# When an attention row's operands are asked for and copied, in a fused attention and MoE kernel

## The chip, the cores and the metric

The kernel runs on one core of a Trainium2 chip. The core has TensorE (PE: matrix products into PSUM), VectorE (DVE), ScalarE (ACT) and GpSimd (POOL), and SyncE (SP), which here only issues DMAs. The metric is the device time of one execution in microseconds, taken as the median over runs; lower is better.

## The reference

The inputs are q, k and v of 8 batch rows x 8 heads x 576 positions x 64, and two weight matrices. Attention is causal within a window: the first four heads see the last 32 positions ("sliding"), the other four every fourth of the last 128 ("dilated"). The result goes through a two-layer network with a squared ReLU.

```python
rel = pos[:, None] - pos[None, :]
mask_plain = (rel >= 0) & (rel < window)                     # window = 32
mask_dil = (rel >= 0) & (rel < window * dilation) & (rel % dilation == 0)   # dilation = 4
scores = np.where(masks, scale * q @ k.T, -1e9)
attn = exp(scores - max) / (sum + 1e-09)
x = (attn @ v).transpose(0, 2, 1, 3).reshape(4608, 512)
h = x @ w_in                                                 # 512 x 2048
r = np.maximum(h, 0.0)
out = (r * r) @ w_out                                        # 2048 x 512
```

## The kernel before

Attention is worked row by row (b = 0 to 7), the network in nine chunks (c = 0 to 8) of 512 tokens. While TensorE works on row b, it also works on chunk b - 1. The order of every engine's instructions is written out by hand: `moe_gen` is a Python generator that emits a few matmuls per step, and `pump(n)` takes n steps. So the program alternates a piece of attention with n steps of a chunk. A chunk's first product (L299) has 32 steps; its ReLU is on ScalarE (L322, `rt`), the square on VectorE (L323, `g`). From chunk 2 on the second product (L376, `mm2_strassen_gen`) is built of seven half-size products, with sums of `g` (`gs`) on VectorE; during chunk 1's first product VectorE also makes sums of w_out (`wt`, L349). Chunks 0 and 1 use plain products (L442), and `store` copies each 128 tokens to `ot` and sends it off.

A row's path to TensorE from row 2 on:

- `load_sliding_qk` (L112): GpSimd's DMA queue loads the sliding heads' k and q from fp32 into the fp16 tile `ns`. `keep_dilated_qk` (L207) copies the dilated heads' k and q to a fp16 DRAM tile `dd`.
- `by_token` (L120) reorders `ns` into `nr`, on VectorE, for row 2 on GpSimd. `keep_sliding_qk` (L217) writes `nr` to a DRAM tile `dp`.
- `transpose_sliding` (L225) and `transpose_dilated` (L229) bring `dp` and `dd` back transposed, as `QKTp` and `QKTd`; each has two buffers, by the row's parity.
- v is loaded by SP into `sv` and `sd` (L132, L137), cast by GpSimd into `vp` and `vd` (L169, L177). A block of queries also needs the end of the block ahead, its halo: copied between partitions by ScalarE for rows 0 and 1 (`halo_sliding` L184, `halo_dilated` L189), by an SP DMA from row 2 on (L194, L197).

`attn_scores` (two sliding parts, two dilated) makes the scores (L562, L581), ScalarE their exponential, VectorE the mask (L552, L553). After each part it may call a hook, then pumps. `attn_values` multiplies by v (sliding L611, dilated L627); VectorE normalizes each product (`rcp`, `xs`, `xd`, L594 and L599). The PSUM tiles of scores and products share a pool of two buffers (`pa`), so a third product waits for the normalization of the first. For rows 2 and 3 (as 0 and 1) `x` is transposed on TensorE; from row 4 on `attn_values_by_dma` has SP transpose it (L669, L676), and calls `then[0]` and `then[1]` on the way.

In the loop over b, before:

- `after_transposes(b)` has GpSimd read one element of row b's transposed tile, so that its queue waits for the transposes to land; then GpSimd asks for row b + 1's `ns` and `dd`. So these are asked for at the start of row b's work.
- The hook behind the fourth score part (`turn`) copies `ns` to `nr`, writes `dp` and loads row b + 1's `sv`.
- For b of 4 and more, `turned` (behind two dilated products) transposes `dp`; `done` (behind the fourth) transposes `dd`, loads `sd`, has GpSimd wait for the last transposed x (L854), cast `sv` and lets SP move the sliding halo.

Each engine runs its queue in order, and an SP or GpSimd DMA waits where it stands for its operands. The tag "n" of `natp` has two buffers, taken in turn by `ns` and `nr`; `otp` has three.

Of the kernel before, what the change touches and what calls it, by code (L numbers as in the profile page):

```python
# [13 lines left out]
P = 128  # L14
# [3 lines left out]
def kernel(  # L18
# [9 lines left out]
    nc = tc.nc  # L28
# [88 lines left out]

    def by_token(b, n):
        r = natp.tile([P, 9, HH, D], FP16, name=f"nr{b}", tag="n")
        (nc.gpsimd if b == 2 else nc.vector).tensor_copy(  # L120
            r.rearrange("x j h d -> x h j d"), n.rearrange("x h (j d) -> x h j d", d=D)
        )
        return r
# [15 lines left out]
    def load_v(b):  # L139
        load_sliding_v(b)  # L140
        load_dilated_v(b, nc.sync)
# [90 lines left out]
    seen = const.tile([P, 1], FP16, name="seen")  # L232

    def after_transposes(b):
        t = QKTp[b % 2][:, 0, 1, PADP : PADP + 1] if b == 2 else QKTd[b % 2][:, 0, 1, KPAD : KPAD + 1]
        nc.gpsimd.tensor_copy(seen, t)


    nsd = {0: load_qk(0)}
# [208 lines left out]
        )  # L448

    halves = {}  # L450

    def store(c, t, po):
        if t % 2 == 0:
            halves[c] = otp.tile([P, 2, DM], FP32, name=f"ot{c}_{t}", tag="ot")
        ot = halves[c][:, t % 2]
        nc.scalar.copy(ot, po)
        (nc.sync if c else nc.gpsimd).dma_start(out=out[(c * 4 + t) * P : (c * 4 + t + 1) * P, :], in_=ot)

    def mm2_gen(c, g):
        for t in range(TOKC // P):  # L460
# [40 lines left out]
    def pump(n):  # L501
        for _ in range(n):
            while pending:
                try:
                    next(pending[0])
                    break
                except StopIteration:
                    pending.pop(0)
# [92 lines left out]
    def x_tiles(b):  # L601
        x = xp.tile([QB, 2, NB, 2, D], FP16, name=f"xs{b}", tag="xs")
        return x, [xp.tile([QD[t], DIL, HH, D], FP16, name=f"xd{b}_{t}", tag=f"xd{t}") for t in range(2)]
# [18 lines left out]
    def av_dilated(b, t, a, xs):  # L622
        pav = pa(f"paw{b}_{t}_{a}")
        for e in range(2):
            for h in range(HH):
                off = e * 288 + a * CL + Q0D[t]
                nc.tensor.matmul(  # L627
                    pav[:, e, h * (D + 2) : h * (D + 2) + D + 1],
                    AT[:, 4 + h, off : off + P],
                    vd[b % 2][:, t, 2 * a + e, h, 0 : D + 1],  # L630
                    start=True,
                    stop=True,
                )
        normalize(b, f"d{t}_{a}", pav, QD[t], xs[1][t][:, 2 * a : 2 * a + 2])
# [26 lines left out]
    def x_from(b, t, y):  # L661
        t0 = b * S % XW + DIL * Q0D[t]
        o = xT[:, 2:4, t0 : t0 + DIL * QD[t]].rearrange("x c (i r) -> x c i r", r=DIL)
        nc.scalar.copy(o, y.rearrange("x r c i -> x c i r"))  # L664
# [16 lines left out]
    def attn_scores(b, gap, less=0, hooks={}):  # L681
        for hp in range(2):
            s_sliding(b, hp)
            if hp in hooks:
                hooks[hp]()
            pump(gap)
        for g in range(2):
            s_dilated(b, g)
            if 2 + g in hooks:
                hooks[2 + g]()  # L690
            if g and b < 2:
                halo_sliding(b, 0)
            pump(gap - less)

    def attn_values(b, gap, wide=False, hooks={}):
        xs = x_tiles(b)
        for mp in range(3):
            av_sliding(b, mp, xs)
            if b < 2:
                if mp < 2:  # L700
                    halo_sliding(b, mp + 1)
                else:
                    halo_dilated(b, 0)
            pump(gap)
        x_sliding(b, 0, xs, wide)
        if b < 2:
            halo_dilated(b, 2)
        pump(gap)
        av_dilated(b, 0, 0, xs)
        pump(gap)  # L710
        x_sliding(b, 1, xs, wide)
        pump(gap)
        av_dilated(b, 0, 1, xs)
        pump(gap)
        for a in range(2):
            av_dilated(b, 1, a, xs)
            pump(gap)
        x_dilated(b, 0, xs, wide)
        pump(gap)
        x_dilated(b, 1, xs, wide)  # L720

    def attn_values_by_dma(b, then):
        xs = x_tiles(b)
        for mp in range(3):
            av_sliding(b, mp, xs)
            pump(3)
        x_sliding_by_dma(b, xs)
        ys = []
        for t in range(2):
            for a in range(2):  # L730
                av_dilated(b, t, a, xs)
                pump(4 + 2 * (a > t))
            if t == 0:
                then[0]()
            ys.append(x_dilated_by_dma(b, t, xs))
        then[1](ys[1])
        pump(6)
        x_from(b, 0, ys[0])
        pump(7)
        x_from(b, 1, ys[1])  # L740

# [35 lines left out]
    load_v(1)  # L777
    cast_sliding_v(1)
    load_w_out((3,))
    cast_dilated_v(1)  # L780
    ns = load_sliding_qk(2)
    dd = keep_dilated_qk(2)
    nr = by_token(2, ns)
    for mp in (1, 2):
        av_sliding(0, mp, xs)
        pump(1)
# [26 lines left out]
        t_dilated(1, m, a, True)  # L813
        pump(2)
    attn_scores(1, 2, 1)
    attn_values(1, 1, True)
    pump(1000)
    dp = keep_sliding_qk(2, nr)
    transpose_dilated(2, dd)
    transpose_sliding(2, dp)  # L820
    load_v(2)


    for b in range(2, B):
        pending.append(moe_gen(b - 1))
        nxt = b + 1
        hooks = {}
        if nxt < B:
            after_transposes(b)
            ns = load_sliding_qk(nxt)  # L830
            if b == 2:
                cast_v(b)
                halo_sliding_by_dma(b)
                halo_dilated_by_dma(b)
            dd = keep_dilated_qk(nxt)
        if b > 4:
            cast_dilated_v(b)
            halo_dilated_by_dma(b)
        kept = []

        def turn():
            kept.append(keep_sliding_qk(nxt, by_token(nxt, ns)))
            load_sliding_v(nxt)

        def turned():
            if nxt < B:
                transpose_sliding(nxt, kept[0])

        def done(y):
            if nxt < B:  # L850
                transpose_dilated(nxt, dd)
                if b > 3:
                    load_dilated_v(nxt, nc.sync)
                    nc.gpsimd.tensor_copy(seen, y[:, 0, 0, 0:1])  # L854
                    cast_sliding_v(nxt)
                    halo_sliding_by_dma(nxt)

        if nxt < B:
            hooks[3] = turn
        pump({2: 24, 3: 16}.get(b, 3))  # L860
        attn_scores(b, 4 if b == 2 else 3, 0, hooks)
        if b < 4:
            load_dilated_v(nxt, nc.sync)
            turned()
            done(None)
            cast_v(nxt)
            halo_sliding_by_dma(nxt)
            halo_dilated_by_dma(nxt)
            attn_values(b, b)
        else:  # L870
            attn_values_by_dma(b, (turned, done))
        pump(1000)
    pending.append(moe_gen(B - 1))
    pending.append(moe_gen(B))
# [31 lines left out]
```

## Time and profile before

| what | value |
|---|---|
| median of 13 runs | 309.73 us (307.33 to 314.84) |
| profiled execution: its time, its span | 307.95 us, 306.2 us |
| TensorE busy | 287.3 us (94%) |
| VectorE, ScalarE, GpSimd busy | 207.7, 170.5, 66.9 us |
| L299, first product, 640 matmuls | 134.0 us busy |
| `nr` copy: VectorE, GpSimd | 0.76 us (median of 5), 2.10 us (1) |
| `ns` loads, asked for to landed | 3.9 to 14.8 us, median 7.2 us |
| granted TensorE clock | 1.00 |

The profile is of one execution. A row of a timeline has the start in us, the duration in us, the engine, the line, the operation and its tiles (out<-in); in brackets stands how long the engine was idle before it and what ended that. A row of the chain has the start, the duration and the piece. Kernel stages: rows 0 and 1 and the weights until about 61 us, row 2 with chunk 1 until 95, row 3 with chunk 2 until 127, row 4 until 159, row 5 until 189, row 6 until 220, row 7 until 250, then chunks 7 and 8.

### The profile page before, as it was taken

To read this page: it belongs to the slowest core of one execution; us is meant where nothing else is said; L and a number is where in the kernel's file an instruction comes from. 1 tells how busy PE (TensorE), PEld (TensorE's weight loads), DVE (VectorE), ACT (ScalarE), POOL (GpSimd) and SP (SyncE) were. 2 spreads that over 40 slices of the span, in tenths; PEclk is the share of its full clock that TensorE was granted. 3 is DMA by queue.
4 is the path that set the end of the run, shared out by engine and by line. 5 is a ranking of instruction groups with operands and counts; after the bars stand their busy time and mean duration, and the time that the engine had idled before them with its cause. 6 is when DMAs were issued, how large, how long until landed. Compare 5 with 4: busy or idle time off the path is not lost.

```text
span 306.2 us, 6889 instructions
## 1 busy us (share of the span) xinstructions
PE 287.3 (94%) x2762; PEld 192.2 (63%) x2762; DVE 207.7 (68%) x433; ACT 170.5 (56%) x288; POOL 66.9 (22%) x117
## 2 busy tenths in 40 slices
PE   1898998999799999998999999999999999999994
PEld 0554554555355568754888987558755975785583
DVE  7784448568852698478939993899399834734652
ACT  1766648678335863494349535952595346426620
POOL 4571018413705301330044004400230000000000
PEclk9999999999999999999999999999999999999999
DMA  7899997999899989999989999999942330003004
GB/s 118 168 216 215 206 182 117 177 257 200 142 216 210 213 162 195 178 232 207 145 174 274 202 139 177 270 201 139 180 160 41 40 130 8 2 1 139 0 0 139
DMA packets 77520, 47.25 MB, mean 154 GB/s; under 512 B 58544, under 2 KB 69296, under 8 KB 77488
## 3 DMA queue, kind: packets, MB, share of 16 engines
q1 hardware_dynamic: 68416, 32.13, 50.9%
q0 software_dynamic: 9072, 14.68, 27.0%
q8 instruction: 21, 0.34, 0.5%
q14 instruction: 11, 0.09, 0.1%
HBM read 36.70 MB, written 16.52 MB: 174 GB/s over the span
## 4 chain that ended last, share of the span: by engine, by line
PE 67%; DMA 19%; DVE 4%; SPq 3%; ACT 2%; issue 2%; POOL 2%; POOLq 0%; DVEq 0%
PE ph L299 24%; PE pa L376 15%; DMA ns<-in_q_dram 12%; PE po L442 8%; PE pb L376 7%; DMA QKTd<-dd 4%; PE pc L376 3%; PE paw L627 3%; DMA sv<-in_v_dram 2%; PE pav L611 2%; PE pf L496 2%; DMA vp<-vp 2%; SPq L225 1%; SPq L229 1%; ACT AT L552 1%
## 5 line engine op out<-in xcount | busy, mean ns | idle before, releaser
L299 PE MATMUL ph<-xT,wi 128*128 128x512 f16 (+1 forms) x640 | 134.0, 359 | 0.7 <-ACT xT L664 0.7
L322 ACT ACTIVATE rt<-ph 128x512 f16<-128x512 f32 x144 | 86.2, 612 | 46.8 <-PE ph L299 40.6
L299 PEld LDWEIGHTS <-wi 128*128 128x128 f16 x640 | 68.3, 114 | 46.0 <-issue 0.6
L323 DVE TENSOR_TENSOR g<-rt 128x512 f16<-128x512 f16 x144 | 61.9, 443 | 37.7 <-ACT rt L322 37.0
L376 PEld LDWEIGHTS <-g 128*128 128x128 f16 x448 | 43.3, 98 | 6.1
L376 PEld LDWEIGHTS <-gs 128*128 128x128 f16 x336 | 31.9, 98 | 4.5 <-DVE gs L333 0.7
L442 PE MATMUL po<-wo,g 128*128 128x512 f16 x128 | 33.1, 380 | 0.0
L403 DVE TENSOR_TENSOR ov<-pb,ov 128x512 f32<-128x512 f32 x14 | 9.7, 692 | 30.7 <-PE pb L376 17.3
L376 PE MATMUL pa<-wt,gs 128*128 128x256 f16 x224 | 27.5, 273 | 0.0
L376 PE MATMUL pb<-wt,g 128*128 128x256 f16 x224 | 27.1, 273 | 0.0
L169 POOL CAST vp<-sv 128x512 f16<-128x512 f32 x24 | 14.5, 637 | 51.3 <-DMA sv<-in_v_dram 51.3
L177 POOL CAST vd<-sd 128x512 f16<-128x512 f32 (+1 forms) x32 | 22.1, 719 | 9.8 <-PE ph L299 5.2
L392 ACT COPY ov<-pa 128x512 f32<-128x512 f32 x14 | 8.2, 585 | 27.1 <-PE pa L376 27.1
L553 DVE TENSOR_TENSOR AT<-AT,maskp 128x576 f16<-128x576 f16 x32 | 19.6, 628 | 4.7 <-ACT AT L552 3.5
L599 DVE TENSOR_TENSOR xd<-paw,rcp_d 80x512 f16<-80x512 f32 (+1 forms) x32 | 21.9, 685 | 1.1
L552 ACT ACTIVATE AT<-pz 128x576 f16<-128x576 f32 x32 | 19.9, 707 | 1.7 <-PE pz L581 1.6
L552 ACT ACTIVATE AT<-ps 128x576 f16<-128x576 f32 x32 | 19.2, 660 | 1.3 <-PE ps L562 0.8
L392 ACT COPY ou<-pa 128x512 f32<-128x512 f32 x14 | 8.2, 586 | 16.6 <-PE pa L376 16.6
L599 DVE TENSOR_TENSOR xs<-pav,rcp_p 96x512 f16<-96x512 f32 x24 | 16.5, 687 | 0.8
L611 PEld LDWEIGHTS <-AT 128*128 128x128 f16 x192 | 9.0, 98 | 11.4 <-issue 5.9
L627 PEld LDWEIGHTS <-AT 128*128 128x128 f16 x256 | 11.9, 98 | 5.6 <-PE paw L627 1.3
L442 PEld LDWEIGHTS <-g 128*128 128x128 f16 x128 | 10.3, 97 | 8.1
(83 smaller groups left out, 280.1 us busy)
## 6 DMA issues: line engine op xcount, KB each, us to landing
sv<-in_v_dram SPq DMA_DIRECT2D x14, 288.0 KB, 5.7
dp<-nr SPq DMA_DIRECT2D x12, 288.0 KB, 4.0
out_dram<-ou SPq DMA_DIRECT2D x6, 512.0 KB, 3.7
out_dram<-ov SPq DMA_DIRECT2D x6, 512.0 KB, 4.6
sd<-in_v_dram SPq DMA_DIRECT2D x8, 320.0 KB, 5.3
ns<-in_k_dram POOLq DMA_DIRECT2D x8, 288.0 KB, 6.8
ns<-in_q_dram POOLq DMA_DIRECT2D x8, 288.0 KB, 7.9
sd<-in_v_dram SPq DMA_DIRECT2D x8, 256.0 KB, 6.3
```

What stands on the lines that cost most here:

```text
L177: nc.gpsimd.tensor_copy(vd[b % 2][p0:P, t, c : c + 2, :, 0:D], sd[p0:P, t, :, D * c : D * (c + 2)].rearrange("p h (c d) -> p c h d", d=D),)
L299: nc.tensor.matmul(ph[:, t0:t1], wi4[ffc // 4][:, dmk, :, ffc % 4], xT[:, dmk, x0 : x0 + t1 - t0], start=(dmk == 0 and t0 == 0), stop=(dmk ...
L322: nc.scalar.activation(rt, ph[:], ACTF.Relu)
L323: nc.vector.tensor_mul(g[:, ffc, :], rt, rt)
L376: nc.tensor.matmul(banks[bank][:, t], a(k, t), b(k), start=(new and t == 0 and k == 0), stop=(k == HF - 1), skip_group_check=True,)
L392: nc.scalar.copy(ot, banks[A])
L442: nc.tensor.matmul(po, g[:, ffc, t * P : (t + 1) * P], wo[ffc // 4][:, ffc % 4, :], start=(ffc == 0), stop=(ffc == NFF - 1),)
L552: nc.scalar.activation(AT[:, u, 0:UW], ps[:, :, 0 : UW // 2], ACTF.Exp, scale=scale)
L553: nc.vector.tensor_mul(AT[:, u, 0:UW], AT[:, u, 0:UW], mask)
L599: nc.vector.tensor_tensor(out=x, in0=pv, in1=rb, op=ALU.mult)
L611: nc.tensor.matmul(pav[:, i, h * (D + 2) : h * (D + 2) + D + 1], AT[:, 2 * (h // 2) + m // 3, off : off + P], vp[b % 2][:, m, h, 0 : D + 1 ...
L627: nc.tensor.matmul(pav[:, e, h * (D + 2) : h * (D + 2) + D + 1], AT[:, 4 + h, off : off + P], vd[b % 2][:, t, 2 * a + e, h, 0 : D + 1], st ...
```

## The change

Row 2's copy to `nr` moves from GpSimd to VectorE, in row 1's `attn_values` behind the first dilated product; its `ns` is asked for ahead of row 1's dilated casts. Row 2's sliding operands are transposed ahead of the dilated ones. Chunk 0's results no longer leave by GpSimd's queue as each is done: they are kept, and SP sends them as two stores of 512 KB behind the loads of row 2's v. Row 2's halo is copied by ScalarE, as for rows 0 and 1. Row 2's scores begin behind 18 steps of chunk 1 (24 before), row 3's behind 12 of chunk 2 (16), with 4 steps between its parts (3).

From row 5 on, `ns` and `dd` are asked for within the row ahead (`ask`): row 5's in row 3's work behind row 4's casts, row 6's and 7's in `done`, behind the casts of `sv`, with no wait for the transposes. The copy (`turn`) hangs behind the third score part in row 4 and the second in rows 5 and 6 (before: the fourth). `turned` goes ahead of the sliding products.

```diff
 def by_token(b, n):
-        (nc.gpsimd if b == 2 else nc.vector).tensor_copy(
+        nc.vector.tensor_copy(
...
+    def leave_first():
+        for t, o in first_out:
+            nc.sync.dma_start(
+                out=out[t * P : (t + 2) * P, :].rearrange("(t p) m -> p t m", p=P), in_=o
+            )
...
-        (nc.sync if c else nc.gpsimd).dma_start(out=out[(c * 4 + t) * P : (c * 4 + t + 1) * P, :], in_=ot)
+        if c:
+            nc.sync.dma_start(out=out[(c * 4 + t) * P : (c * 4 + t + 1) * P, :], in_=ot)
+        elif t % 2:
+            first_out.append((t - 1, halves[c]))
...
-            if g and b < 2:
+            if g and b < 3:
                 halo_sliding(b, 0)
...
     load_w_out((3,))
+    ns = load_sliding_qk(2)
     cast_dilated_v(1)
-    ns = load_sliding_qk(2)
     dd = keep_dilated_qk(2)
-    nr = by_token(2, ns)
...
-    attn_values(1, 1, True)
+    attn_values(1, 1, True, lambda: dp.append(keep_sliding_qk(2, by_token(2, ns))))
     pump(1000)
-    dp = keep_sliding_qk(2, nr)
+    transpose_sliding(2, dp[0])
     transpose_dilated(2, dd)
-    transpose_sliding(2, dp)
     load_v(2)
+    leave_first()
...
+    def ask(b):
+        if b < B:
+            nss[b] = load_sliding_qk(b)
+            dds[b] = keep_dilated_qk(b)
+
+    def turn(b):
+        if b < B:
+            dps[b] = keep_sliding_qk(b, by_token(b, nss[b]))
+            load_sliding_v(b)
+
+    for b in range(2, 4):
...
+        after_transposes(b)
+        nss[nxt] = load_sliding_qk(nxt)
+        if b == 2:
+            cast_v(b)
+        dds[nxt] = keep_dilated_qk(nxt)
+        pump(18 if b == 2 else 12)
+        attn_scores(b, 4, 0, {3: lambda: turn(nxt)})
...
+        if b == 3:
+            ask(nxt + 1)
+        attn_values(b, b)
+        pump(1000)
+
+    for b in range(4, B):
...
+        def done(y):
+            if nxt < B:
+                transpose_dilated(nxt, dds[nxt])
+                load_dilated_v(nxt, nc.sync)
+                nc.gpsimd.tensor_copy(seen, y[:, 0, 0, 0:1])
+                cast_sliding_v(nxt)
+                ask(nxt + 1)
...
+        pump(3)
+        attn_scores(b, 3, 0, {2 if b == 4 else 1: lambda: turn(nxt)})
+        attn_values_by_dma(b, (turned, done, ahead))
```

## The prediction

> **What bounds the kernel now.** I began with the page: TensorE's busy row against the span.
>
> ```profile
> span 306.2 us, 6889 instructions
> PE 287.3 (94%) x2762; PEld 192.2 (63%) x2762; DVE 207.7 (68%) x433; ACT 170.5 (56%) x288; POOL 66.9 (22%) x117
> ```
>
> TensorE lacks 19 us of the span. Windows of 0 to 25 us (15.73 busy) and 250 to 306.2 (51.83 busy) hold 13.6 of it, and the change leaves the work there alone. The chain from 249.75 us on is nearly all TensorE, so time saved earlier reaches the end undiminished. Next, TensorE's timeline, for instructions with idle time in brackets:
>
> ```profile
> 82.25 0.29 PE L611 MATMUL pav<-vp,AT 128*128 128x65 f16 x4 [1.74 <-DMA vp<-vp]
> 113.39 0.41 PE L611 MATMUL pav<-vp,AT 128*128 128x65 f16 x8 [0.57 <-DVE xs L599]
> 140.45 0.41 PE L611 MATMUL pav<-vp,AT 128*128 128x65 f16 x8 [1.32 <-DVE xs L599]
> 201.38 0.41 PE L611 MATMUL pav<-vp,AT 128*128 128x65 f16 x8 [0.60 <-DVE xs L599]
> ```
>
> With 0.23 and 0.54 near 50 us these are all the gaps over 0.15 us after 25 us: 5.0 us. The first is row 2 waiting for its halo by DMA. The rest are rows 3, 4 and 6: the third sliding product needs a PSUM buffer of two, which VectorE frees by normalizing the first. VectorE's timeline says why that is late:
>
> ```profile
> 138.38 0.76 DVE L120 COPY nr<-ns 128x2304 f16<-128x2304 f16 x1 [1.80 <-DMA ns<-in_q_dram]
> 168.66 0.76 DVE L120 COPY nr<-ns 128x2304 f16<-128x2304 f16 x1 [0.61 <-issue]
> 199.31 0.76 DVE L120 COPY nr<-ns 128x2304 f16<-128x2304 f16 x1 [1.09 <-DMA ns<-in_q_dram]
> ```
>
> VectorE stands in order at the copy of the next row's q and k, which have not landed. GpSimd's timeline shows when they were asked for, and the chain what each load then took:
>
> ```profile
> 155.12 0.19 POOL L854 COPY seen<-yd 128x1 f16<-128x1 f16 x1 [22.39 <-DMA yd<-xd]
> 155.25 1.73 POOL L169 CAST vp<-sv 128x512 f16<-128x512 f32 x3
> 158.90 0.19 POOL L236 COPY seen<-QKTd 128x1 f16<-128x1 f16 x1 [1.92 <-DMA QKTd<-dd]
> 159.47 0.66 POOL L112 DMA_DIRECT2D ns<-in_k_dram  x1 [0.38 <-issue]
> ```
>
> ```profile
> 131.01 7.34 DMA ns<-in_q_dram
> ...
> 160.11 7.94 DMA ns<-in_q_dram
> ...
> 190.27 9.01 DMA ns<-in_q_dram
> ```
>
> So the bound is TensorE, with about 4.2 us of waits in reach of this edit (1.74 + 0.57 + 1.32 + 0.60).
>
> **The change, part by part.** Offsets are from before's own times.
>
> *Chunk 1, row 2's copy.* GpSimd's copy took 2.10 us at 55.50; VectorE's row is 0.76. It stands behind the first dilated normalization, ending at 56.1, where VectorE idled 0.60 until 56.75; so it costs TensorE at most 0.1. Its operand is asked for 2.7 us earlier (ahead of the 2.76 us of dilated casts), so it should be there by 54.5. But those casts slide from 47.15 to 48.4, onto the dilated masks, which finished at 52.06; their lateness can stall the third sliding product at 53.10. Bounds 0 and 0.5; I take **+0.2**, since two of four masks are touched.
>
> *SP before row 2.* dp leaves at 57.0 instead of 57.63, landing 3.5 and 4.3 later (the shortest and longest of rows 4 to 7 are 3.1 and 4.4). Before, the four stores of chunk 0 (4 x 256 KB from GpSimd's queue at 58.06 to 62.13) flew along: the second dp took 6.3, QKTd 6.8 and 7.7, against a median 3.6 for QKTd later. Without them: sliding transposes issued 60.5 and 62, dilated 63.3 and 64.6 (1.3 us each), landed by 66 and 69; v from 66 instead of 69.16, landing about 72 (75.27 before); sd by 75. Row 2's scores start 6 pump steps earlier (24 steps took 61.04 to 71.49, 0.435 each): 61.04 + 18 x 0.435 = 68.9, sliding needed then, dilated at 73.3. Both are in time, by 3 and 4 us.
>
> *Row 2's halo by ScalarE.* Five copies (rows 0.40 to 0.62 us) replace two DMAs (4.64 landing). The DMA needed all of vp; ScalarE's first copy needs one cast and stands behind the last exponential, done near 77.4; TensorE needs it at 77.8. **The 1.74 goes.** What comes next? ScalarE must also finish one activation and the second copy by the second product at 78.9: 77.8 + 0.6 + 0.55 = 78.95. And row 2's scores now all lie within chunk 1's first product: VectorE has per cycle (2.2 us of TensorE) two masks 0.74, two squares 0.68, one weight sum 0.60, together 2.02, back to back. That fits, but GpSimd's casts (72 to 76.5) fall here entirely. VectorE's row under a cast:
>
> ```profile
> 74.74 0.42 DVE L323 TENSOR_TENSOR g<-rt 128x512 f16<-128x512 f16 x1
> 75.08 1.23 DVE L553 TENSOR_TENSOR AT<-AT,maskp 128x576 f16<-128x576 f16 x2
> 76.24 0.82 DVE L323 TENSOR_TENSOR g<-rt 128x512 f16<-128x512 f16 x1
> 76.99 1.09 DVE L349 TENSOR_TENSOR wt<-wo,wt 128x1024 f16<-128x1024 f16 x1
> ```
>
> About 1.4 us was lost in 3.9 us of casts. The Trainium skill ("SBUF: State Buffer", Who interferes with whom) is harsher: a VectorE instruction with two SBUF inputs and a GpSimd one reading SBUF exclude each other entirely. By the rule 4.4 us of casts cost up to 4.4, less 0.7 of slack (4 x 0.18); by the row 1.6 less 0.7. I take the row: VectorE about 0.9 late, first normalization at 79.5 + 0.9 = 80.4 against 80.2 needed. With ScalarE's lateness, **0.6** new stall, bounds 0.1 and 4.7 (the next paragraph's). Row 2 nets -1.1.
>
> *Row 3's q and k.* They must land before VectorE's copy at 77.5. Asked for when QKTd is seen, 69.0. Chunk 0's stores (1 MB, now 69.2 on SP, behind v) compete. The Trainium skill ("DMA: Bandwidth & Descriptors", Queues, rings and completion order): a DMA engine takes turns between queues by packet. By that, ns (576 KB) shares evenly with sd and the stores: at about 200 KB/us (212 and 187 in the windows 70 to 74 and 74 to 78 us), from 72.5 on (3.5 after asking), done 72.5 + 2 x 2.9 = 78.3. By order of asking, the 1 MB goes first: 5 us later, 83; copy, square and normalization (0.7, 0.34, 0.83) end at 84.9 and the stall is 4.7. The trace has turns: sd and ns, asked for within 2 us, landed at 77.1, 79.1, 80.3, 80.9. I take 78.3; the wait of 0.8 is the slack that the casts would have eaten, so it is inside the 0.6.
>
> *Row 3* (pump 12, gap 4): scores take 4 x 2.11 us instead of 4 x 1.77, for the same masks and sums plus two squares (0.7), so VectorE gains about 0.7 against TensorE. Its 0.57 goes: **-0.5**. Row 4's operands land near 100, needed at 106.
>
> *Row 4.* ns(5) and dd(5) leave behind row 4's casts near 124 instead of 130.37, so land by 132; the copy now stands behind the third score near 132.4. **-1.3**. What is late next: QKTd(4), in flight then (before: landed 129.67, asked for 126.07), may lose up to 2 of its 3 us of lead. Nothing.
>
> *Rows 5 and 6.* The wait for QKTd is dropped, so ns leaves right behind the casts: 157.0 for 159.47, and 187.4 for 189.62. But the copy moves two scores ahead: behind the second sliding masks, done 165.5 and 195.7. Landing, if the 0.63 and 7.94 (9.01) stay: 166.1 and 197.1. Behind the copy now stand square, masks, squares, masks, square, reciprocal and normalization, 3.7 us back to back; TensorE wants the first normalization at 170.4 and 200.6, so ns may land until 166.0 and 196.1. Stall 0.1 and 1.0, where 0 and 0.60 were; with shared engines slowing sd a little, **+0.2 and +0.4**. Bounds: -0.6 (lands 1 us sooner) to +4 together (nothing gained in landing: 168.6 and 199.3).
>
> *Costing nothing:* QKTp's transposes ahead of xs's on SP: dp lands at about 170.5 to 172, transposes end before the 173.2 at which xs is normalized; cover gone, 2.6 us on x, which is used a chunk later. halo_sliding later in the text keeps its place on SP. Chunk 0's stores hold buffers of otp until about 79; the third is free, the next taken after 86.
>
> Sum: +0.2 -1.1 -0.5 -1.3 +0.2 +0.4 = **-2.1**. The profiled run took 307.95 (1.75 around the span), 1.8 below the median 309.73. Span 304.1, that run 305.9, **median 307.6**.
>
> **Rivals.** *Slower: copies before their data.* At rows 5 and 6 VectorE reaches the copy two scores sooner, with masks behind it, and ns is not there. If landings don't move with the issue (168.6 and 199.3, because the transposes, sd and stores then in flight have first call), the stalls are 168.6 - 166.0 = 2.6 and 199.3 - 196.1 = 3.2 instead of 0.1 and 1.0: +4.7 on my sum, 312.3. For it: in the windows from 155 to 170 us the DMA share is 1.03 to 1.14, so no spare engine time shows. Against: the issue is 2.2 to 2.5 us earlier, and turns between queues favour a small queue. It decides from landings 1 us later than my 166.1 and 197.1 (then the gain of 2.1 is gone); 1.8 later makes the kernel measurably slower. *No change: stall for stall.* Row 2's wait comes back at VectorE, by casts between the row's and the rule's price or by ns(3) at 80.4: a stall of 2.1 and more in place of 0.6, and 6's grows by another 0.6: 309.7. For it: ScalarE and VectorE are both full in row 2's scores. *All waits vanish*: 309.73 - 4.2 = 305.5; needs ns sooner by more than its issue.
>
> **How the numbers follow.** The kernel's runs scatter such that 0.5% (1.5 us) is about what a measurement can tell. Forecast 0.48, its own range 306.3 to 308.8 by the bounds of single terms; all waits vanish 0.08; stall for stall 0.24; slower 0.20. Some seven eighths of the first lie over 1.5 us under 309.73, with the second 0.50 faster; the rest of the first and nearly all of the third give 0.28 same; 0.22 slower. Range: 305.2 to 311.5, which leaves out the lowest few hundredths and the worse two thirds of the slow case.
>
> **What would show it.** Right: no wait for vp by DMA; the copy at row 5 (near 132) without idle; rows 3 and 4's third product without gap; row 2's first v landed near 72; no store of chunk 0 before 69. Wrong: idle over 2 us before the copies of rows 3, 6 or 7, ending with ns; gaps ended by ScalarE's vp copies at row 2; TensorE waiting for QKTd at row 4.

## The result: 1.55% slower, and the profile after

The changed kernel takes 314.61 us (median of 11 runs, 312.09 to 316.27), the kernel before 309.77 us on the same chip (median of 48). The ratio is 1.0155, with a 95% interval of 1.0125 to 1.0186. It is 4.8 us slower, where 2.1 us less was forecast (307.6 us, range 305.2 to 311.5). Medians below are over all runs of a kernel; ratios leave out disturbed runs, so the two can differ by up to 0.4%.

The profiled execution took 318.43 us, 3.8 us more than the median. Its first load of q took 5.89 us (4.96 before), and the work at 27 us stands 2.0 us later (27.00 for 24.99 us); the rest of the 3.8 us is not explained. So the two profiles are compared by their gaps and not by the clock on the page; where a time of row 2 is given "by before's clock", the 2.0 us are taken off.

The page, with the busy time of the engines and the clock that TensorE was granted in 40 slices (before: TensorE 287.3 us busy, clock 9 in every slice):

```profile
span 316.1 us, 6890 instructions
...
PE 291.1 (92%) x2762; PEld 193.7 (61%) x2762; DVE 207.1 (66%) x434; ACT 173.2 (55%) x293; POOL 61.5 (19%) x109
...
PEclk9999999999899999987999999999999999999999
```

The same 2762 matmuls take 3.8 us longer, and in three slices the clock is below full. TensorE's timeline, the rows with idle time over 0.3 us between 60 and 250 us:

```profile
85.48 0.60 PE L620 MATMUL pav<-vp,AT 128*128 128x65 f16 x8 [3.29 <-DVE rcp_p L603]
140.27 0.66 PE L590 MATMUL pz<-QKTd 64*128 64x80 f16 x16 [3.07 <-DMA QKTd<-dd]
180.14 0.42 PE L620 MATMUL pav<-vp,AT 128*128 128x65 f16 x8 [0.49 <-DVE xs L608]
211.88 0.41 PE L620 MATMUL pav<-vp,AT 128*128 128x65 f16 x8 [1.70 <-DVE xs L608]
```

Row by row, the idle time in us:

| row | before | forecast | after |
|---|---|---|---|
| 2 | 1.74, for the halo's DMA | 0.6 | 3.29, for the first sliding normalization |
| 3 | 0.57 | about 0 | 0.28 |
| 4 | 1.32, at the third sliding product | 0 | 3.07, at the third score, for `QKTd` |
| 5 | 0 | 0.1 | 0.49 |
| 6 | 0.60 | 1.0 | 1.70 |

Two gaps decide: row 2's and row 4's. Windows of the trace right behind them show the second cost (columns: window, its length, busy us and count for TensorE, weight load, VectorE, ScalarE and GpSimd, then granted clock, DMA share, GB/s):

```profile
84.00:88.00 4.00, 2.52 (x18) 1.43 (x19) 2.94 (x8) 0.18 (x1) 0.00 (x0) 0.61 1.05 248
...
140.00:144.00 4.00, 3.73 (x38) 1.73 (x38) 1.92 (x4) 2.14 (x4) 0.00 (x0) 0.50 0.75 266
144.00:148.00 4.00, 4.00 (x28) 1.84 (x23) 2.57 (x6) 2.53 (x5) 0.00 (x0) 0.71 0.94 209
```

Once TensorE had stood for 3 us, its clock was halved for 3.4 us at row 2 and for 6.8 us at row 4. Before, with no gap over 1.74 us after 25 us, it stayed at 1.00.

Row 4's holder, in the view of the line that transposes `dd` (SP's queue, its two instructions for row 4):

```profile
L229 SPq DMA_TRANSPOSE QKTd<-dd x2: 1685/1808/1932, 128.1 to 130.1; - x2
...
  PE pz L590: 3.1, 1
...
DMA to landing us min/median/max: 6.0/8.1/10.1
```

The first took 6.0 us and the second 10.1; in the profile before they took 4.5 and 3.6 us. Row 5's q and k had been asked for by GpSimd on both sides of the second transposition at 130.1: `ns` at 129.2 and 129.9, `dd` at 130.5 and 131.0.

Row 2's holder, on VectorE's timeline, with the copies of rows 6 and 7 below:

```profile
74.91 1.24 DVE L562 TENSOR_TENSOR AT<-AT,maskp 128x576 f16<-128x576 f16 x2
76.07 1.58 DVE L322 TENSOR_TENSOR g<-rt 128x512 f16<-128x512 f16 x2
...
79.73 1.58 DVE L322 TENSOR_TENSOR g<-rt 128x512 f16<-128x512 f16 x2
...
83.41 0.76 DVE L120 COPY nr<-ns 128x2304 f16<-128x2304 f16 x1 [0.75 <-issue]
...
175.59 0.76 DVE L120 COPY nr<-ns 128x2304 f16<-128x2304 f16 x1 [2.22 <-DMA ns<-in_q_dram]
207.32 0.76 DVE L120 COPY nr<-ns 128x2304 f16<-128x2304 f16 x1 [3.34 <-DMA ns<-in_q_dram]
```

Two squares take 0.75 us when GpSimd is silent, and 1.58 here. VectorE's work from 74.91 to 81.24 took 6.33 us, against 3.44 by its undisturbed durations: 2.9 us lost in 5.4 us of GpSimd's casts. Then it stood 0.75 us: the row names no cause, but row 3's `ns` landed only at 83.3. The idle times of 2.22 and 3.34 us before the copies of rows 6 and 7 are VectorE's; TensorE's gaps there are the 0.49 and 1.70 of the table.

### The profile page after: what moved, and what is told of

Same layout as the page of the kernel before. It is cut to its first block, busy times and chain, and to the rows that moved or that the text cites. A ratio compares the mean times of both kernels' runs of the same rounds, so it can differ in the third digit from the quotient of the medians.

```text
span 316.1 us, 6890 instructions
## 1 busy us (share of the span) xinstructions
PE 291.1 (92%) x2762; PEld 193.7 (61%) x2762; DVE 207.1 (66%) x434; ACT 173.2 (55%) x293; POOL 61.5 (19%) x109
## 4 chain that ended last, share of the span: by engine, by line
PE 64%; DMA 16%; DVE 13%; issue 2%; POOL 2%; ACT 2%; SPq 1%; DVEq 0%; POOLq 0%
PE ph L298 28%; PE pa L375 12%; DMA ns<-in_q_dram 11%; PE po L441 7%; PE pb L375 6%; DVE AT L562 4%; PE pc L375 3%; DMA QKTd<-dd 3%; DVE g L322 3%; PE paw L636 2%; DVE xs L608 2%; DMA sv<-in_v_dram 1%; PE pav L620 1%; POOL vp L169 1%; DVE nr L120 1%
## 5 line engine op out<-in xcount | busy, mean ns | idle before, releaser
L298 PE MATMUL ph<-xT,wi 128*128 128x512 f16 (+1 forms) x640 | 136.7, 363 | 0.7 <-ACT xT L673 0.7
L375 PEld LDWEIGHTS <-g 128*128 128x128 f16 x448 | 43.3, 98 | 6.1
L441 PE MATMUL po<-wo,g 128*128 128x512 f16 x128 | 33.9, 388 | 0.0
L562 DVE TENSOR_TENSOR AT<-AT,maskp 128x576 f16<-128x576 f16 x32 | 17.2, 556 | 4.6 <-ACT AT L561 3.5
L562 DVE TENSOR_TENSOR AT<-AT,maskd 128x576 f16<-128x576 f16 x32 | 16.2, 540 | 4.6 <-ACT AT L561 4.0
L620 PEld LDWEIGHTS <-AT 128*128 128x128 f16 x192 | 9.2, 99 | 12.9 <-issue 8.6
L620 PE MATMUL pav<-vp,AT 128*128 128x65 f16 x192 | 10.4, 195 | 6.6 <-DVE rcp_p L603 3.3
```

The costliest lines, as they stand in the source:

```text
L298: nc.tensor.matmul(ph[:, t0:t1], wi4[ffc // 4][:, dmk, :, ffc % 4], xT[:, dmk, x0 : x0 + t1 - t0], start=(dmk == 0 and t0 == 0), stop=(dmk ...
L375: nc.tensor.matmul(banks[bank][:, t], a(k, t), b(k), start=(new and t == 0 and k == 0), stop=(k == HF - 1), skip_group_check=True,)
L441: nc.tensor.matmul(po, g[:, ffc, t * P : (t + 1) * P], wo[ffc // 4][:, ffc % 4, :], start=(ffc == 0), stop=(ffc == NFF - 1),)
L562: nc.vector.tensor_mul(AT[:, u, 0:UW], AT[:, u, 0:UW], mask)
L620: nc.tensor.matmul(pav[:, i, h * (D + 2) : h * (D + 2) + D + 1], AT[:, 2 * (h // 2) + m // 3, off : off + P], vp[b % 2][:, m, h, 0 : D + 1 ...
```

## The experiments

The theory after the result has three parts: row 5's early loads cut into row 4's transposition (A in the expectations below), row 2 is held by VectorE, which is late under GpSimd's casts or behind `ns` (B), and the earlier copies of rows 6 and 7, in the work of rows 5 and 6, wait for their data (C). The rival is that the halved clock, not the waits, makes most of the loss. The table has all results. Ratios are to the kernel before on the same chip; a gap of 0 means none over 0.25 us; "first" means the kernel of the first experiment, the changed one with row 5 asked for as before. Four runs (rows 6, 7 as before; before with rows 5 to 7 changed; the two with the copy later in all rows) have only 4 executions each:

| run | median us | ratio (95%) | gaps of rows 2 / 3 / 4 / 5 / 6, us |
|---|---|---|---|
| changed kernel | 314.61 | 1.0155 (1.0125, 1.0186) | 3.29 / 0.28 / 3.07 / 0.49 / 1.70 |
| row 5 asked for as before | 310.77 | 1.0031 (1.0003, 1.0060) | 2.44 / 0.28 / 0.67 / 0.30 / 0.24 |
| rows 6, 7 asked for as before | 313.14 | 1.0101 (1.0059, 1.0143) | 3.15 / 0.27 / 3.28 / 0.51 / 1.48 |
| rows 5 to 7 as before | 310.5 | 1.0037 (1.0014, 1.0059) | 2.58 / 0.28 / 1.02 / 0.77 / 0.88 |
| before, with rows 5 to 7 changed | 315.15 | 1.0173 (1.0125, 1.0221) | 1.44 / 1.30 / 4.95 / 0 / 0 |
| changed, gaps filled | 313.44 | 1.0106 (1.0073, 1.0138) | filled / 0.28 / 1.06 left / 0.63 / 1.31 |
| first, casts held | 310.68 | 1.0009 (0.9985, 1.0033) | 2.58 / 0.28 / 1.79 / 1.36 / 1.86 |
| first, copy later | 316.65 | 1.0189 (1.0111, 1.0267) | row 2: 1.78; new ones |
| before, copy later, halo | 314.68 | 1.0119 (1.0031, 1.0207) | row 2: 0; new ones |
| before, halo alone | 309.21 | 0.9928 (0.9888, 0.9968) | 0.26 / 1.08 / 1.36 / 0.28 / 1.50 |
| before, halo, copy later in rows 2, 3 | 311.5 | 1.0021 (0.9993, 1.0048) | 0 / 0.68 / 3.62 / 0 / 0 |
| first, stores early | 312.55 | 1.0022 (0.9988, 1.0057) | 3.30 / 0.28 / 0.92 / 1.04 / 0.30 |
| first, row 2's start as before | 308.09 | 0.9960 (0.9934, 0.9985) | 0 / 0.28 / 0.74 / 0.85 / 0.53 |
| before, halo, row 3 earlier | 309.07 | 0.9946 (0.9921, 0.9972) | 0.36 / 1.78 / 1.50 / 0 / 0.45 |

### Row 5's loads: asked for as before

```diff
-        if b == 3:
-            ask(nxt + 1)
...
+        if b == 4:
+            after_transposes(b)
+            ask(nxt)
...
-        attn_scores(b, 3, 0, {2 if b == 4 else 1: lambda: turn(nxt)})
+        attn_scores(b, 3, 0, {3 if b == 4 else 1: lambda: turn(nxt)})
```

> The changed kernel with row 5's q and k asked for as before the change: at row 4's start, behind the wait for row 4's transposes, and copied behind the fourth score. Rows 6 and 7, and row 2's part, stay changed. Theory A (the ungated loads slow row 4's dilated transposes: 3.07 us of TensorE idle before row 4's third score, and a clock dip behind it): that gap is gone, QKTd of row 4 lands in about 4 us each instead of 6 and 10, the gap of 1.3 us at row 4's third sliding product is back, and the granted clock rises; 314.6 - 1.75 - 2 to 3 = 310 to 311. Theory B (row 2 under GpSimd's casts is what costs): 313 or more.

It took 310.77 us, 3.8 us less than the changed kernel. The same view of the transposing line, and then TensorE's timeline at row 2:

```profile
L229 SPq DMA_TRANSPOSE QKTd<-dd x2: 1407/1602/1797, 125.6 to 127.4; - x2
...
DMA to landing us min/median/max: 3.4/3.8/4.2
```

```profile
82.68 0.41 PE L620 MATMUL pav<-vp,AT 128*128 128x65 f16 x8 [2.44 <-DVE rcp_p L603]
```

The transpositions are back at 4.2 and 3.4 us, and the wait at the third score is gone; of the old wait at the third product 0.67 is left. Part A is confirmed: taking this one term out takes 3.8 of the 4.8 us away.

### Rows 6 and 7, and rows 5 to 7, asked for as before

```diff
+        if 4 < b < B - 1:
+            after_transposes(b)
+            ask(nxt)
...
-                ask(nxt + 1)
...
-        attn_scores(b, 3, 0, {2 if b == 4 else 1: lambda: turn(nxt)})
+        attn_scores(b, 3, 0, {2 if b == 4 else 3: lambda: turn(nxt)})
```

In the second run the condition is `b < B - 1`, row 5's `ask` in row 3's work is gone too, and the hook is behind the fourth part (3) for every row.

> The changed kernel with rows 6 and 7's q and k asked for behind the wait for the transposes and copied behind the fourth score, as before the change; row 5's early load stays. Theory C (the copies of rows 6 and 7 stand ahead of their data, my slower rival): the gaps of 0.49 and 1.70 us in rows 5 and 6 go back to 0 and 0.6, 314.6 - 1.6 = 313.0. Theories A and B: no more than that, 313 to 314.6, since row 4's and row 2's gaps of about 3 us stay.

> The changed kernel with all of rows 5 to 7's loads and copies as before the change: only row 2's and row 3's part is left (row 2's copy on VectorE, chunk 0's stores behind row 2's v, the halo by ScalarE, the scores started earlier). If A and C hold all of the loss: at or under before, 308.5 to 309.8. By B (row 2's third sliding product waits 3.3 us where 1.7 were, and the clock dips for 3.4 us): 309.8 + 1.6 + 1.7 - 0.5 = 312.6.

With rows 6 and 7 undone alone, the median is 1.5 us lower, on four executions and with intervals that overlap, but rows 5 and 6 still wait 0.51 and 1.48 us: the gaps that C puts down to the early loads and copies did not go. With all three rows undone it is 310.5, the same as with row 5 undone alone (310.77), and between the two forecasts for it. So these runs do not show that the early loads of rows 6 and 7 help or hurt, and C is not borne out.

### The kernel before, with the part for rows 5 to 7 alone

```diff
+        if b == 3:
+            ask(nxt + 1)
...
+                cast_sliding_v(nxt)
+                ask(nxt + 1)
...
+        attn_scores(b, 3, 0, {2 if b == 4 else 1: lambda: turn(nxt)})
+        attn_values_by_dma(b, (turned, done, ahead))
```

Rows 2 and 3 keep the steps, halo and stores of the kernel before.

> The kernel before with rows 5 to 7's loads asked for early and their copies moved, alone; rows 2 and 3 as before. By A and C: 309.8 + (3.1 - 1.3) + 2 to 3 of clock + 1.6 = 315 to 316, with a gap at row 4's third score. By B: about 311 at most. If row 4's transposes leave in time with rows 2 and 3 unchanged, so that they meet row 5's loads less, the gap there is small and the time is 311 to 312.

It took 315.15 us, 1.73% over the kernel before: this part by itself is a loss as large as the whole. TensorE's timeline has it in one row:

```profile
138.70 0.67 PE L581 MATMUL pz<-QKTd 64*128 64x80 f16 x16 [4.95 <-DMA QKTd<-dd]
```

The gap at row 2 stays the halo's DMA (1.44 us), and rows 5 and 6 have none. In this run the second transposition took 11.5 us; row 5's `ns` had been asked for at 126.1, it at 127.0. The pattern holds in all 15 traces: where the first load of `ns` was asked for 0.4 to 0.9 us ahead of row 4's second transposition, it took 10.1 (changed kernel), 10.5 (rows 6, 7 undone), 10.9 (gaps filled) and 11.5 us; in the eleven others, where they were asked for once it had landed, 3.4 to 3.9 us.

The traces also record every DMA packet. The DMA view's two queues (q0 is GpSimd's, q1 SP's: packets, MB, share of 16 engines) in the changed kernel from 132 to 138 us, and then SP's in the kernel before from 126 to 130, while its second transposition flew:

```profile
q0 software_dynamic: 818, 1.14, 105.1%
q1 hardware_dynamic: 416, 0.10, 12.7%
```

```profile
q1 hardware_dynamic: 2491, 0.81, 97.3%
```

A packet of the transposition has 256 bytes, one of `ns` 1152 and one of `dd` 2048. Undisturbed, some 2300 packets passed in these 4 us. In the changed kernel none passed from 132 to 134 us, beside 365 of `ns`; from 135 to 138 it was 287 beside 261 of `dd`, about one for one; and once `dd` was through, the last 716 took 1.1 us. The three other slow transpositions each have a stretch of one for one beside `dd` (192 beside 175, 130 beside 121, 299 beside 250). One for one in packets is one for eight in bytes, so the transposition ends when the loads and copies do. Why it got no turn at all beside `ns` for 2 us is not shown, and as `ns` and `dd` were always moved together, no run says what either would do alone.

### The clock: both gaps filled with matmuls

```diff
+    def fill(n, name):
+        pf = pmool.tile([P, TOKC], FP32, name=name, tag="pm")
+        for _ in range(n):
+            nc.tensor.matmul(pf, ident, maskp[:, 0:TOKC], start=True, stop=True)
...
+        if b == 4:
+            fill(14, "pfs")
...
+            if b == 2 and mp == 2:
+                fill(13, "pfv")
```

These 27 matmuls are extra work in the changed kernel, at the places where TensorE stood; nothing reads their result.

> The changed kernel with products whose result nobody reads (about 3 us of them) put where TensorE would stand still: 13 ahead of row 2's third sliding product, 14 ahead of row 4's third score. Every wait stays. If the granted clock falls because TensorE stood still, and its half speed behind the gaps costs up to half of the 8 us that a mean clock of 0.987 stands for, the clock stays at 1.00 and the time falls by 2 to 4 us, 310.5 to 312.5, though TensorE has 6 us more work. If only the waits cost, 314.6 or a little more.

The clock in the page's slices, where the changed kernel has an 8, another 8 and a 7:

```profile
PEclk9999999999999999999999999999999999999999
```

The median is 313.44 us, 1.2 us less than the changed kernel's; by the ratios it is 0.5% of 309.7, 1.5 us, and the two intervals overlap. That lies between what was expected if the clock cost 2 to 4 us and if it cost nothing. The 13 at row 2 ended about 0.3 us after the wait that they cover (`xs` was done at 82.85 us, TensorE's next product began at 83.19), so the figure is a low one. An upper figure comes from the mean granted clock of the executions: its median is 0.989 in the changed kernel, 0.998 with the gaps filled and 0.998 in the kernel before, and 0.9% of 312 us is an estimated 2.8 us, if TensorE had work in all of the half-speed time. So the half clock makes some 1.5 to 2.8 of the 4.8 us, and the waiting the rest. The rival is not refuted as to size, for the clock may make half of the loss; but the clock falls because TensorE waits, since with the gaps filled it did not fall in the median execution.

### What holds row 2

Three runs on the first experiment's kernel (row 5 as before) each take one suspect away. First, row 2's four dilated casts are held until its masks are made:

```diff
-            cast_v(b)
+            cast_sliding_v(b)
...
+        if b == 2:
+            nc.gpsimd.tensor_copy(seen, AT[:, 7, 0:1])
+            cast_dilated_v(b)
```

> The kernel with row 5's loads gated (310.8), with row 2's four dilated casts on GpSimd held back until row 2's masks are done, so that only the three sliding casts fall on VectorE's masks, squares and sums. Theory: VectorE loses about half of the time that a cast runs (2.9 us in 5.4). With the dilated casts (3.0 us) gone it is 1.5 us sooner, and the gap before row 2's third sliding product (2.44 us in that profile) falls to about 1, with no or a smaller clock dip: 308.5 to 309.5. If ns(3)'s landing holds it instead, the gap stays within 0.5 us of 2.4: 310.8.

VectorE's timeline: the later squares are at 0.75 us for two again, the masks are done at 79.7, and then it stands until `ns` has landed (at 80.7):

```profile
77.58 0.75 DVE L322 TENSOR_TENSOR g<-rt 128x512 f16<-128x512 f16 x2
...
78.86 0.82 DVE L562 TENSOR_TENSOR AT<-AT,maskd 128x576 f16<-128x576 f16 x2
80.86 0.86 DVE L120 COPY nr<-ns 128x2304 f16<-128x2304 f16 x1 [1.19 <-issue]
```

The gap stays at 2.58 us. The waiting is passed on from the casts to the landing.

Second, the copy goes behind the second sliding product in rows 2 to 6, so that row 2's first two normalizations need no `ns`. In rows 2 and 3 the loads, transpositions and casts for the next row go there with it, and in rows 4 to 6 the transpositions of `dp` go behind those of the sliding x; the cut below leaves these lines out:

```diff
+            if mp == 1 and mid:
+                mid()
...
-        attn_scores(b, 4, 0, {3: lambda: turn(nxt)})
+        attn_scores(b, 4)
+
+        def all_next():
+            turn(nxt)
...
+        attn_values(b, b, mid=all_next)
...
+            if mp == 1:
+                then[3]()
...
-        attn_scores(b, 3, 0, {3 if b == 4 else 1: lambda: turn(nxt)})
-        attn_values_by_dma(b, (turned, done, ahead))
+        attn_scores(b, 3)
+        attn_values_by_dma(b, (turned, done, ahead, lambda: turn(nxt)))
```

> The kernel with row 5's loads gated (310.8), with VectorE's copy of the next row's operands in rows 2 to 6 behind the second sliding normalization, so that the third sliding product waits for no copy. Row 2's gap loses the copy's 0.75 us (VectorE is late by casts as well), the gaps of 0.3 to 0.7 in rows 3 to 6 go: 310.8 - 0.75 - 1.4 = 308.6, and less if row 2's dip of the clock goes too (307). If row 3's or a later row's transposes now come too late, a gap at its scores shows instead and nothing is won.

Row 2's gap falls to 1.78 us, and now the casts alone hold it (two masks took 1.65 us at 77.49). But the kernel takes 316.65 us, with new gaps in rows 4 to 6. TensorE's timeline has the first two, the third is 2.18 us at 224.41; ScalarE's timeline is that at the first:

```profile
158.23 1.91 PE L375 MATMUL pa<-wo,gs 128*128 128x256 f16 x16 [2.13 <-ACT ov L391]
190.62 3.38 PE L375 MATMUL pa<-wo,gs 128*128 128x256 f16 x16 [2.30 <-ACT ov L391]
```

```profile
156.43 1.26 ACT L673 COPY xT<-yd 128x640 f16<-128x640 f16 x1 [4.08 <-DMA yd<-xd]
157.60 0.57 ACT L391 COPY ov<-pa 128x512 f32<-128x512 f32 x1
```

ScalarE stands 4.08 us for the x that SP transposes; behind it in its queue is the copy that empties a bank for TensorE's next product. The same move on the kernel before (with row 2's halo by ScalarE, and no other part of the change) gave the same picture:

```diff
+            if mp == 1 and mid:
+                mid()
...
+            if mp == 1:
+                then[2]()
...
-        if nxt < B:
-            hooks[3] = turn
...
-            attn_values_by_dma(b, (turned, done))
+            attn_values_by_dma(b, (turned, done, turn if nxt < B else lambda: None))
```

> The kernel before, with two edits only: the copy behind the second sliding normalization in rows 2 to 6, and row 2's halo copied by ScalarE. Chunk 0's stores, row 2's copy on GpSimd, the start of the scores and the wait for the transposes stay as before. The gaps of 1.74, 0.57, 1.32 and 0.60 us should go: 309.5 - 4 = 305.5; if VectorE under the casts keeps 1 us of row 2's gap, 306.5.

It took 314.68 us. Row 2 has no gap at its third sliding product there, and 1.94, 2.44 and 2.55 us stand ahead of the same product in rows 4 to 6.

Third, chunk 0's stores leave by GpSimd's queue as each is done, as before:

```diff
-        if c:
-            nc.sync.dma_start(out=out[(c * 4 + t) * P : (c * 4 + t + 1) * P, :], in_=ot)
-        elif t % 2:
-            first_out.append((t - 1, halves[c]))
+        (nc.sync if c else nc.gpsimd).dma_start(out=out[(c * 4 + t) * P : (c * 4 + t + 1) * P, :], in_=ot)
...
-    leave_first()
```

> The changed kernel with row 5's q and k asked for as before (the first experiment) and chunk 0's results leaving by GpSimd's queue as each is done, as before. If row 2's gap of 2.4 us is the late landing of row 3's q and k behind those stores: they land 2 to 3 us after asking sooner (near 78 instead of 81), the gap falls to 1.2 us or less, time 1 us or more under the first experiment's 310.8. If VectorE's time lost under GpSimd's casts holds it alone: the gap stays at 2.0 to 2.5 us, 310.3 to 311.5. The stores then fly beside row 2's transposes: these may land 3 us later, with a gap for QKTp at row 2's start of up to 1 us.

It did not help: the ratio is 1.0022 where it was 1.0031, `ns` took 9.5 us with the stores out of its way and 9.6 with them, and the gap is 3.30 us. The stores are not what makes it late.

What is common to all of these is that row 2's scores start 6 steps of chunk 1 sooner. So the start was put back, with all else of the first experiment kept:

```diff
-        pump(18 if b == 2 else 12)
+        pump(24 if b == 2 else 12)
```

> The first experiment (the changed kernel with row 5's q and k asked for as before) with row 2's scores begun behind 24 steps of chunk 1, as before, in place of 18. If row 2's gap comes from its early start (2.6 us sooner, while row 3's q and k and the casts of v are no sooner): the 2.4 us gap falls to 0.5 us or less, time about 308.5, ratio 0.994 to 0.998. If VectorE's time lost under the casts moves along and holds it as before: a gap of 1.5 us or more stays, 310.5 to 311, ratio 1.000 to 1.004.

It took 308.09 us, a ratio of 0.9960. TensorE's timeline from 54 to 115 us has two rows with idle time over 0.25 us, in rows 1 and 3, and none in row 2:

```profile
54.64 0.41 PE L620 MATMUL pav<-vp,AT 128*128 128x65 f16 x8 [0.71 <-DVE rcp_p L603]
113.06 0.41 PE L620 MATMUL pav<-vp,AT 128*128 128x65 f16 x8 [0.28 <-DVE xs L608]
```

The 6 steps are row 2's cause. They move its need for the first normalization 2.6 us ahead, while the casts of v and row 3's `ns`, which both have to be done by then, come no sooner. Either alone then holds it for about 2 us (1.78 by the casts, 2.58 behind `ns`), which is why taking one away left the gap.

### Parts of the change on the kernel before

Row 2's halo by ScalarE alone:

```diff
-            if g and b < 2:
+            if g and b < 3:
...
-                halo_sliding_by_dma(b)
-                halo_dilated_by_dma(b)
```

> The kernel before with one part of the change: row 2's halo copied by ScalarE. If the DMA for vp was the only thing that held row 2 (my term of -1.1 to -1.7): the 1.74 us gap goes, no more than 0.6 us comes in its place, the other rows stay as they were (0.6, 1.3, 0.6), ratio 0.994 to 0.997. If VectorE, late under the casts and behind the copy of row 3's q and k, only takes the wait over: a gap of 1.5 us or more ended by VectorE's normalization, ratio 0.999 to 1.003.

The ratio is 0.9928: 0.7% is 2.2 us (1.0 to 3.5 by the interval, on 9 executions), and row 2's gap fell from 1.74 to 0.26. (The profiled execution, 2.7 us over the median, also waited 1.54 us for `QKTp` at row 2's start.)

With rows 3 and 4 copied later in addition (the `mid` of above, in rows 2 and 3 only):

```diff
+            if mp == 1 and mid:
+                mid()
...
-        if nxt < B:
+        if 3 < b and nxt < B:
             hooks[3] = turn
```

> The run before this one with rows 3 and 4's q and k copied behind the second sliding product in rows 2 and 3 as well (in rows 4 to 6 as before). These rows transpose x on TensorE, so that no x is late on SP's queue. If it is only SP's transposes of x that made the later copy costly: rows 2 and 3 without gaps (before: 1.74 and 0.57), row 4's 1.3 stays, no new gap ended by ScalarE's copies, ratio 0.991 to 0.995. If the later copy makes row 3's or 4's transposed operands late: a gap over 1 us ended by QKTp or QKTd at the start of row 3 or 4, ratio 0.998 to 1.004.

The rival's size came true, at another place. Rows 2 and 3 are free of the old gaps (row 3 has one of 0.68 us, for `gs`), but row 4's operands landed 1.3 us later (130.96 for 129.67), hence row 5's `ns` was asked for later, and row 4's copy, still behind the fourth score, stood for it. VectorE's and TensorE's timelines:

```profile
140.19 0.76 DVE L120 COPY nr<-ns 128x2304 f16<-128x2304 f16 x1 [4.10 <-DMA ns<-in_q_dram]
```

```profile
142.27 0.42 PE L611 MATMUL pav<-vp,AT 128*128 128x65 f16 x8 [3.62 <-DVE xs L599]
```

Last, row 3's earlier start on top of the halo alone:

```diff
-        pump({2: 24, 3: 16}.get(b, 3))
-        attn_scores(b, 4 if b == 2 else 3, 0, hooks)
+        pump({2: 24, 3: 12}.get(b, 3))
+        attn_scores(b, 4 if b < 4 else 3, 0, hooks)
```

> The kernel before with row 2's halo by ScalarE, and row 3's scores begun behind 12 steps of chunk 2 with 4 steps between (before: 16 and 3). If my term for row 3 holds (VectorE gains 0.7 us): row 3's gap (0.57 in the profile before, 1.08 with the halo alone) falls under 0.3, ratio 0.990 to 0.993. If the early start only brings row 3 ahead of its data, as at row 2: a gap over 1 us at its third sliding product, ratio 0.994 to 0.999.

```profile
113.81 0.41 PE L611 MATMUL pav<-vp,AT 128*128 128x65 f16 x8 [1.78 <-DVE xs L599]
```

Row 3's gap grew, to 1.78 us, and the ratio is 0.9946, no better than the halo alone. By itself the earlier start brings row 3 ahead of its data too (a cause read from the traces, not tried): row 4's `ns` landed at 111.3, the copy wanted it 1.4 us sooner. In the run with row 2's start put back it landed at 109.0 and the copy had no idle time: it had been asked for 1.7 us sooner (101.99 for 103.73), because row 3's transpositions landed sooner (100.65 for 102.31).

## Why the prediction was wrong

The sum was -2.1 us; by the medians it is +4.8. The forecast's rival of a slower kernel had the direction right, at 0.20 and 312.3 us, but named the copies of rows 6 and 7, which was not the cause. Two of its own signs of being wrong came: TensorE waited for `QKTd` at row 4, and VectorE idled over 2 us before the copies of rows 6 and 7. Step by step:

- **Row 4, the step that failed.** "QKTd(4), in flight then ... may lose up to 2 of its 3 us of lead. Nothing." The second transposition lost 6.5 us (10.1 for 3.6) and TensorE stood 3.07. The 1.32 that the step took away did go (VectorE's copy at 142.33 had no idle time). Net +1.75 in place of -1.3, and with the clock behind it 3.8 us between the run that undoes it and the changed kernel. The lead of 3 us was known, the price of sharing was guessed at 2, and nothing of it was carried into the sum or the range. The near rows of before were not used: `QKTd` of row 2 beside chunk 0's stores had taken 6.8 and 7.7 us, as the forecast itself says, and the transpositions of `dp` for rows 3 and 4, with loads of v ahead of them in the same queue, 6.0 to 8.1. Each is 2.4 us or more over `QKTd`'s 3.6, up to more than the whole lead. How the time was lost the packets show: none or one of 256 bytes for each of up to 2048 beside it. The forecast had no sum for this; for row 3's `ns` it took turns as equal bytes.
- **Row 2, the other.** The 6 steps were tested against row 2's own operands, "both in time, by 3 and 4 us", which was right: v landed 71.2 us by before's clock (forecast near 72), and TensorE did not wait for `QKTp`. They also set the time at which VectorE must have made the masks under the casts and copied row 3's `ns`, and there the new stall was put at 0.6 us, where 2.44 (row 5 undone) to 3.29 were measured. Both terms were too small. Of the casts' cost the row of before was taken, 1.4 us in 3.9, so 1.6 for 4.4 us of casts from 72 on; 2.9 us were lost in 5.4, from 73.1 to 79.0 by before's clock. The Trainium skill's rule ("SBUF — State Buffer", Who interferes with whom), full exclusion, would be 5.4: per us of casts 0.36 by the row, 0.54 measured, 1 by the rule, so the trace's row was the better guide and still too low. `ns` was put at 78.3 by turns between queues ("DMA: Bandwidth & Descriptors", Queues, rings and completion order), and landed at 81.3 by before's clock, 10.9 us after it was asked for (at 80.2, 9.6 us, with row 5 undone). By the trace's packets its data moved from 72.3 to 79.3 by before's clock, and from 74.1 to 79.8 with row 5 undone, where the sum had 72.5 to 78.3. So its share was roughly right (7.0 and 5.7 us for 5.8). The other error was a landing 2.0 us after the last data packet in the first run, and a start 1.6 us later in the second; why, no run shows. The step's first half, "The 1.74 goes", was right: the halo alone is worth some 2.2 us.
- **The clock was not foreseen.** A gap was counted at its own length. The page "TensorE: Matmul & The Clock Gate", Part 1, puts the window of the gate at about 3.4 us, and the trace shows stretches at half speed of 3.4 and 6.8 us behind gaps of 3.3 and 3.1. Filling the gaps won 1.2 to 1.5 us, and by the mean clock they cost up to 2.8.
- **Row 3, -0.5:** -0.29 measured, right in direction. The reason given (VectorE gains on TensorE) is not enough: the earlier start alone made row 3's gap longer (1.78 us), and it was short only where `ns` landed sooner.
- **Rows 5 and 6, +0.2 and +0.4:** +0.49 and +1.10 in the profile, and near nothing in the medians (rows 6 and 7 undone on top of row 5 change 0.3 us). The landings took 9.3 and 10.0 us, where 7.9 and 9.0 stood in the sum. The rival that expected 4.7 us from them does not fit these runs.
- **Chunk 1's copy, +0.2:** no new gap in the changed kernel's profile, but 1.06, 0.57, 0.28 and 0.71 us in four of the eight others that have this part (rows 5 to 7 as before, casts held, copy later, row 2's start as before). It comes in some executions and not in others.

Seen from the other end, 308.1 us with both failed steps undone becomes 310.8 with the 6 steps (+2.7 by the medians, +2.2 by the ratios) and 314.6 with row 5's early loads on top (+3.8). The 6 steps were not undone on the changed kernel itself, so whether the two add up in the other order is not shown. Without these two the rest of the change is faster than the kernel before by 0.4% (0.15 to 0.66), which is no more than the halo alone brought.

## What to carry to other kernels

When a load is asked for earlier, look at what is in flight on the same DMA engines and who waits for that, above all a transposition with a lead of a few us. Reckon its share in packets, not in bytes: here it lasted until the loads and copies beside it had landed. When a piece of work is started sooner, list everything that must be done by its end, not only its own operands; what does not move with it becomes the wait, and taking away one of two such waits shows nothing. A gap of 2 to 3 us on TensorE may have a stretch at half clock behind it; the next section says when it did.

## What the runs showed of the hardware

Row 4's DMA transpositions landed in 3.4 to 4.8 us where row 5's loads were not yet asked for; with the first load of `ns` asked for just ahead of the second, it took 10.1 to 11.5 us, in each of four kernels, and landed within 1.5 us of the last copy of `dd` (140.1 beside 138.7, 138.7 beside 138.9, 138.6 beside 137.8, 137.5 beside 136.7). While copies of `dd` flew, its 256-byte packets passed about one for one with their 2048-byte ones (287 beside 261 in 3 us).

The length of a gap on TensorE does not tell whether its clock falls: a gap of 2.18 us was followed by half clock in one run, and one of 3.62 us in another was not. The records of the granted clock in the 15 traces tell more. Leaving out the last stretch of each trace, every one at half clock lasts 3.41 or 6.83 us, and every one at full clock a multiple of 3.41 (30.7, 51.2 and 71.7 are 9, 15 and 21 times 3.413). So the clock changes on a fixed grid of 3.41 us, whenever the gap begins. The falls go with how long TensorE was busy within one stretch of the grid. After 26 us, all eleven stretches at full clock with up to 1.31 us of busy time were followed by half clock, of the two with 1.37 and 1.38 us one was, and of those with 1.46 us or more none. The gap of 3.29 us in the changed kernel left 0.72 us busy from 81.47 to 84.88; the one of 3.62 us fell on two stretches and left 1.46 and 1.74. Busy time is not all of it: at 22 to 26 us, among row 0's products, two runs (stores early; halo alone) had 2.1 us busy and half clock behind it.
